# Another written-out order for the opening of a fused attention and SwiGLU kernel

## The chip, the cores and the metric

The kernel runs on one core of a Trainium2 chip. A core has a matrix engine (TensorE, PE in the profile; its weight loads are PEld), a vector engine (VectorE, DVE), a scalar engine (ScalarE, ACT), a general one (GpSimd, POOL) and a queue processor (SyncE, SP) that issues the transfers. Each engine takes its instructions in the order in which the program gives them and waits where one needs something that isn't there yet. Sixteen DMA engines move the data. The metric is the device time of one execution in microseconds, as the median of several runs.

## The reference

Windowed causal attention is followed by a gated feed-forward block, both in float32:

```python
batch, n_heads, seq, head_dim = (8, 8, 576, 64)
scores = scale * np.matmul(q, k.transpose(0, 1, 3, 2))
mask = (rel >= 0) & (rel < window)          # rel = query - key, window = 64
attn = exp(scores - max) / sum              # masked scores at -1e9
x = (attn @ v).transpose(0, 2, 1, 3).reshape(4608, 512)
g = x @ w_gate                              # 512 -> 1536
out = (g * sigmoid(g) * (x @ w_val)) @ w_out    # 1536 -> 512
```

q, k and v are 9.4 MB each, the three weight matrices 3.1 MB each.

## The kernel before

**Tiles.** The 4608 tokens are 36 groups of 128 (ORDER); four groups make a tile of 512 tokens, t = 0 to 8. A block n holds the q or k of groups 2n and 2n + 1; v is loaded by group. Weights come in slices s of 256 columns, wg and wv (gate and value) of 512 KB each; slice s serves the output blocks m = 2s and 2s + 1 of the hidden layer. All matrix work is in bf16, so every load is followed by a cast. Loads are named in short below: q3 is q of block 3, v4 is v of group 4, wg5 and wv5 are the gate and value slices 5, wo5 the output slice 5.

**The parts of a group.** `load` (L89), `load1` (L101) and `load_vg` (L110) issue loads of q, k and v; `cast_k` casts to bf16; `turn2` turns a block of q or k by 16 TensorE transposes (L170) and copies the result out of PSUM, `turn1` does it by DMA (L155). `scores` (L207) multiplies keys and queries; with masked=True it adds 16 matmuls that put a large negative number where the mask is off (L215), without it `weigh` has to multiply by a 0/1 mask on VectorE (L229) after the exponential on ScalarE (L227). `cast_v` makes three copies of a group's v: vo as it is, and ve shifted by half a group, which also serves the next group. `products` (L245) multiplies by v, `norm` divides by the row sums (L255, L256), `turn_x` transposes the result on TensorE (L269) and copies it into xT on ScalarE (L270); `turn_x1` does the same by DMA (L277).

**The feed-forward part.** `weights` (L284) and `weights_o` (L292) load slices, `cast_w` and `casts_o` cast them (L120 or L118, on the engine that is named). `step(t, m, c0, n)` computes hidden block m of tile t for n of its 512 tokens: four matmuls into g_ps, four into v_ps (L309), and tanh on ScalarE (L314). `finish()` takes the oldest open step and makes its hidden values on VectorE (L320, L321); only then are its two PSUM buffers free, and there are two of each. `project(t, s)` multiplies by w_out (L327) and stores 128 tokens. `warm(n)` issues n matmuls on zeros.

**What sets the order.** Nothing is planned at run time: the order of the calls is the order on each engine. The opening, some 250 calls written out one by one between `begin()` and the loop, brings in the weights, does the attention of the first groups and all of tiles 0 and 1 but the projection of tile 1. Behind it a loop over w works on tile t while it projects tile t - 1. All loads are issued by SP, so the order of the load calls is the order of the transfers. PSUM tiles of scores, products, transposes and projections rotate through four buffers (ps_a); staging has two buffers for each of q, k and v and six for weight slices.

Of the kernel before, what the change touches and what calls it, by code (L numbers as in the profile page):

```python
# [17 lines left out]
def kernel(  # L18
# [55 lines left out]
    dve, pool, act, sp = nc.vector, nc.gpsimd, nc.scalar, nc.sync  # L74
# [262 lines left out]
    def warm(n):  # L337
        w_ps = ps_f.tile([P, 512], FP32, name="w_ps", tag="g")
        for _ in range(n):
            nc.tensor.matmul(w_ps[:], wz[:, 0:P], wz[:])  # L340

    def begin():

        dve.memset(wz[:], 0.0)
        make_identity(nc, identb[:])
        dve.memset(masks[0][:], 1.0)
        dve.memset(minus[0][:], 0.0)
        pool.affine_select(
            out=masks[0][:], in_=masks[0][:], compare_op=ALU.is_ge, fill=0.0,
            base=64, pattern=[[0, 2], [1, 64]], channel_multiplier=-1,  # L350
        )
# [27 lines left out]
    begin()
    load(0, q, "q_f")  # L380
    load(0, k, "k_f")
    cast_k(0, "q_f", (act, dve))
    load(1, k, "k_f")
    load_vg(0)
    cast_k(0, "k_f", (act, pool))
    load_vg(1)
    warm(11)
    turn2(0, "q_f", (act, dve))
    warm(4)
    turn2(0, "k_f", (act, dve))  # L390
    cast_k(1, "k_f", (dve, act))
    warm(3)
    scores(1)
    load(1, q, "q_f")
    cast_v(0, (dve, pool, pool))
    scores(0, True)
    cast_k(1, "q_f", pool)
    load(2, k, "k_f")
    cast_v(1, (dve, None, None))
    weigh(1)  # L400
    load(2, q, "q_f")
    weigh(0)
    warm(6)
    products(0)
    load_vg(2)
    load_vg(3)
    weights(5, 0)
    load_vg(4)
    norm(0)
    keys_before(1)  # L410
    turn2(1, "k_f", (act, dve))
    warm(4)
    turn_x(0)
    turn2(1, "q_f", (act, dve))
    products(1)
    warm(1)
    scores(2, True)
    cast_k(2, "k_f", pool)
    norm(1)
    cast_k(2, "q_f", dve)  # L420
    weigh(2)
    warm(1)
    scores(3, True)
    weigh(3)
    weights(5, 1)
    load_vg(5)
    turn2(2, "q_f", act)
    load(3, k, "k_f")
    cast_v(2, (dve, pool, pool))
    keys_before(2)  # L430
    turn2(2, "k_f", dve)
    turn_x(1)
    warm(2)
    products(2)
    load(3, q, "q_f")
    norm(2)
    cast_v(3, (act, pool, pool))
    warm(1)
    scores(4, True)
    weights(0, 0)  # L440
    weigh(4)
    products(3)
    norm(3)
    cast_v(4, (act, pool, pool))
    warm(1)
    turn_x(2)
    warm(2)
    turn_x(3)
    weights(0, 1)
    scores(5, True)  # L450
    products(4)
    cast_w(5, 1, pool)
    cast_v(5, pool)
    weigh(5)
    cast_w(5, 0, dve)
    step(0, 10, 0, 256)
    norm(4)
    weights(4, 0)
    step(0, 10, 384, 128)
    turn_x(4)  # L460
    products(5)
    load_vg(6)
    finish()
    keys_before(3)
    cast_k(3, "k_f", (act, pool))
    weights(4, 1)
    norm(5)
    finish()
    step(0, 11)
    cast_k(3, "q_f", (dve, act))  # L470
    load_vg(7)
    turn_x(5)
    turn2(3, "k_f", (dve, act))
    turn2(3, "q_f", (act, dve))
    load(4, k, "k_f")
    cast_w(0, 0, pool)
    finish()
    step(1, 11, 0, 256)
    cast_w(0, 1, act)
    scores(6, True)  # L480
    load(4, q, "q_f")
    finish()
    load_vg(8)
    scores(7)
    step(0, 0)
    weigh(6)
    step(1, 0, 0, 256)
    cast_w(4, 0, pool)
    finish()
    finish()  # L490
    weigh(7)
    cast_w(4, 1, act)
    cast_v(6, pool)
    step(0, 1)
    cast_v(7, (act, pool, pool))
    products(6)
    step(0, 8)
    norm(6)
    cast_k(4, "k_f", (act, pool))
    products(7)  # L500
    turn_x(6)
    finish()
    norm(7)
    weights(3, 0)
    step(0, 9)
    cast_k(4, "q_f", (act, pool))
    cast_w(3, 0, pool)
    weights(1, 0)
    finish()
    weights(3, 1)  # L510
    weights(1, 1)
    keys_before(4)
    load_vg(9)
    finish()
    turn_x(7)
    cast_w(3, 1, pool)
    turn2(4, "k_f", (dve, act))
    turn2(4, "q_f", act)
    step(1, 8)
    finish()  # L520
    step(1, 1)
    weights(2, 0)
    load(5, q, "q_f")
    cast_w(1, 0, pool)
    finish()
    scores(8)
    cast_w(1, 1, pool)
    scores(9)
    weigh(8)
    weights_o(4)  # L530
    load(5, k, "k_f")
    step(1, 10)
    finish()
    cast_w(2, 0, pool)
# [12 lines left out]
    step(0, 7)
    cast_v(8, act)
    step(1, 3)
    finish()  # L550
    cast_k(5, "k_f", (act, pool))
    step(1, 9)
    cast_v(9, (dve, pool, pool))
    finish()
    cast_w(2, 1, pool)
    turn2(5, "q_f", act)
    step(0, 3)
    weights_o(2)
    load_vg(10)
    weights_o(0)  # L560
    finish()
    casts_o(1, pool)
    finish()
    step(0, 10, 256, 128)
    products(9)
    casts_o(4, pool)
    products(8)
    step(0, 4)
    norm(9)
    casts_o(5, pool)  # L570
    finish()
    finish()
    turn2(5, "k_f", act)
    cast_v(10, pool)
    load_vg(11)
    step(1, 2)
    norm(8)
    finish()
    weights_o(3)
    step(0, 5)  # L580
    load1(6, k, "k_f")
    casts_o(0, pool)
    load_vg(12)
    finish()
    scores(10)
    load(7, k, "k_f")
    scores(11)
    casts_o(2, pool)
    casts_o(3, dve)
    weigh(11)  # L590
    turn_x1(8)
    keys_before(6)
    weigh(10)
    cast_k(6, "k_f", pool)
    step(1, 7)
    step(1, 11, 256, 256)
    finish()
    turn_x(9)
    project(0, 3)
    cast_v(11, (pool, dve, act))  # L600
    load1(6, q, "q_f")
    turn1(6, "k_f")
    load1(7, q, "q_f")
    finish()
    cast_k(6, "q_f", (act, pool))
    turn1(6, "q_f")
# [114 lines left out]
```

The softmax here doesn't subtract the row's maximum and nothing guards it: scores larger than these inputs give would overflow.

## Time and profile before

| | |
|---|---|
| median of 4 runs | 339.31 us (338.38 to 339.42) |
| the profiled execution | 339.34 us, of which its span is 337.6 us |
| busy share of the span | PE 97%, PEld 48%, DVE 68%, ACT 45%, POOL 30% |
| SP's transfers | 56.51 MB on queue q1, 76.9% of 16 engines' span |
| TensorE clock | 0.999 of full |

The page divides the span into 40 slices with the busy share of each engine in tenths. The opening ends at 89 us, where the loop's first step starts; the loop fills the rest. "Idle before, releaser" says how long an engine waited ahead of an instruction and what let it go. The DMA share is the mean over 16 engines; where one engine is late and the others are done, it is small although a transfer is still running. A load's time to landing runs from the start of its issue on SP to the moment when whoever waits for it may go. Instructions themselves are fetched by DMA too, on queues of their own (q8, q14).

### The profile page before, as it was taken

How to read it: one execution, taken by the hardware profiler on the slowest of the kernel's cores; microseconds unless marked ns; L12 is line 12 of the kernel's file. 1: busy time of each engine (PE TensorE's matmuls, PEld its weight loads, DVE VectorE, ACT ScalarE, POOL GpSimd, SP SyncE). 2: the span in 40 equal slices, each digit the busy share in tenths (PEclk: the TensorE clock that was granted, in tenths of full speed). 3: DMA queues.
4: the chain of work that ended last, by engine and by line, in shares of the span. 5: the costliest groups of instructions: out<-in, count | busy, mean ns of one | idle time of the engine just before them, and what ended most of it. 6: DMA issues, size and time to landing. Idle time of an engine off the chain costs nothing.

```text
span 337.6 us, 7271 instructions
## 1 busy us (share of the span) xinstructions
PE 326.3 (97%) x2743; PEld 162.5 (48%) x2784; DVE 228.0 (68%) x486; ACT 150.9 (45%) x266; POOL 102.8 (30%) x150
## 2 busy tenths in 40 slices
PE   8887999999999999999999999999999999999996
PEld 3565554555444444444444444444444444444444
DVE  3786898896476767767676665866665866655520
ACT  3595866555534343434343434434343434233222
POOL 4354554842333333333333333223333110000000
PEclk9999999999999999999999999999999999999999
DMA  8999999969988989788989997999796520211014
GB/s 206 263 266 305 266 324 340 316 137 172 242 170 175 167 177 165 145 199 148 192 155 188 133 203 146 177 170 190 144 194 145 119 63 34 63 33 31 31 46 111
DMA packets 151155, 56.98 MB, mean 169 GB/s; under 512 B 125264, under 2 KB 145104, under 8 KB 151120
## 3 DMA queue, kind: packets, MB, share of 16 engines
q1 hardware_dynamic: 151120, 56.51, 76.9%
q8 instruction: 22, 0.36, 0.5%
q14 instruction: 13, 0.11, 0.1%
HBM read 37.75 MB, written 9.44 MB: 140 GB/s over the span
## 4 chain that ended last, share of the span: by engine, by line
PE 87%; DMA 8%; issue 1%; SPq 1%; POOL 1%; ACT 0%; DVE 0%; ACTq 0%; POOLq 0%
PE g_ps L309 27%; PE o_ps L327 27%; PE v_ps L309 27%; DMA v_f<-in_v_dram 4%; PE ao_ps L245 3%; DMA q_f<-in_q_dram 3%; PE s_ps L207 2%; SPq L89 1%; PE tp L170 1%; DMA kT<-k_fb 1%; DMA out_dram<-os__4939 1%; POOL ve L120 1%; PE xtp L269 0%; DVE sg L320 0%; ACT os__4939 L332 0%
## 5 line engine op out<-in xcount | busy, mean ns | idle before, releaser
L320 DVE SCALAR_TENSOR_TENSOR sg<-th,g_ps 128x512 f32<-128x512 f32 (+1 forms) x112 | 74.4, 664 | 56.8 <-ACT th L314 56.5
L309 PE MATMUL g_ps<-xT,wg 128*128 128x512 bf16 (+2 forms) x416 | 110.0, 372 | 2.0 <-DVE sg L320 0.3
L309 PE MATMUL v_ps<-xT,wv 128*128 128x512 bf16 (+2 forms) x445 | 110.9, 371 | 0.9 <-POOL wv L120 0.8
L314 ACT ACTIVATE th<-g_ps 128x512 f32<-128x512 f32 (+1 forms) x112 | 65.1, 584 | 77.5 <-PE g_ps L309 76.0
L327 PE MATMUL o_ps<-wo,hT 128*128 128x512 bf16 (+2 forms) x454 | 98.4, 368 | 0.2
L321 DVE TENSOR_TENSOR hT<-sg,v_ps 128x512 bf16<-128x512 f32 (+1 forms) x112 | 74.9, 669 | 12.4 <-PE v_ps L309 1.0
L309 PEld LDWEIGHTS <-wv 128*128 128x128 bf16 x448 | 43.4, 98 | 50.9 <-POOL wv L120 1.1
L327 PEld LDWEIGHTS <-hT 128*128 128x128 bf16 x456 | 43.6, 98 | 49.2
L309 PEld LDWEIGHTS <-wg 128*128 128x128 bf16 x448 | 40.9, 98 | 43.7 <-issue 0.3
L227 ACT ACTIVATE E<-s_ps 128x512 bf16<-128x512 f32 x72 | 38.8, 598 | 10.0 <-PE s_ps L207 8.6
L120 POOL CAST q_fb<-q_f 128x1024 bf16<-128x1024 f32 (+1 forms) x15 | 14.9, 991 | 70.0 <-DMA q_f<-in_q_dram 58.3
L120 POOL CAST k_fb<-k_f 128x1024 bf16<-128x1024 f32 (+1 forms) x17 | 15.9, 934 | 60.3 <-DMA k_f<-in_k_dram 55.7
L120 POOL CAST ve<-v_f 64x512 bf16<-64x512 f32 x49 | 30.7, 626 | 8.2 <-DMA v_f<-in_v_dram 5.4
L256 DVE TENSOR_TENSOR x_b<-ao_ps,r 128x256 bf16<-128x256 f32 x72 | 30.5, 424 | 2.5
L229 DVE TENSOR_TENSOR E<-E,mask 128x512 bf16<-128x512 bf16 x60 | 26.8, 478 | 7.9 <-ACT E L227 7.3
L120 POOL CAST vo<-v_f 128x512 bf16<-128x512 f32 x24 | 15.2, 633 | 6.2 <-DMA v_f<-in_v_dram 6.2
L245 PEld LDWEIGHTS <-E 128*64 128x64 bf16 x576 | 11.5, 110 | 8.3 <-issue 5.9
L255 DVE RECIPROCAL r<-ao_ps 128x4 f32<-128x4 f32 x72 | 12.5, 173 | 1.2 <-PE ao_ps L245 1.2
L207 PEld LDWEIGHTS <-kT 64*128 64x128 bf16 x512 | 9.9, 95 | 6.8 <-issue 3.4
L245 PE MATMUL ao_ps<-ve,E 128*64 128x65 bf16 x256 | 12.4, 196 | 0.4 <-POOL ve L120 0.2
L245 PE MATMUL ao_ps<-vo,E 128*64 128x65 bf16 x256 | 12.5, 196 | 0.0
L207 PE MATMUL s_ps<-qT,kT 64*128 64x64 bf16 x512 | 12.2, 191 | 0.3 <-ACT qT L118 0.3
(99 smaller groups left out, 149.0 us busy)
## 6 DMA issues: line engine op xcount, KB each, us to landing
v_f<-in_v_dram SPq DMA_DIRECT2D x32, 256.0 KB, 4.6
q_f<-in_q_dram SPq DMA_DIRECT2D x20, 256.0 KB, 4.4
k_f<-in_k_dram SPq DMA_DIRECT2D x18, 256.0 KB, 4.2
k_f<-in_k_dram SPq DMA_DIRECT2D x7, 512.0 KB, 6.9
q_f<-in_q_dram SPq DMA_DIRECT2D x6, 512.0 KB, 5.2
w_f<-in_moe_w_gate_dram SPq DMA_DIRECT2D x6, 512.0 KB, 7.5
w_f<-in_moe_w_val_dram SPq DMA_DIRECT2D x6, 512.0 KB, 7.6
wo_f<-in_moe_w_out_dram SPq DMA_DIRECT2D x6, 512.0 KB, 7.9
```

What stands on the lines that cost most here:

```text
L120: eng.tensor_copy(y, x)
L207: nc.tensor.matmul(ps[a][:, p, b], keys, qT[g // 2 % QR][y, p, o:o + 64], tile_position=(64 * a, 0), start=True, stop=not masked,)
L227: act.activation(e, x[:], AF.Exp, scale=0.125)
L229: dve.tensor_mul(e, e, mk[:].unsqueeze(1).to_broadcast([P, 4, 2, 64]))
L245: nc.tensor.matmul(o_ps[64 * b:64 * b + 64, i, :], Es[g % ER][:, y, b], z[:, y, :], tile_position=(0, 64 * b),)
L255: dve.reciprocal(r[:], o_ps[:, :, D])
L256: dve.tensor_mul(xb[g][:, 256 * h:256 * h + 256].rearrange("r (y d) -> r y d", y=4), o_ps[:, :, 0:D], r[:].unsqueeze(2).to_broadcast([P, 4 ...
L309: nc.tensor.matmul(ps[:, 0:n], w[:, c, P * m:P * m + P], xT[t][:, c, c0:c0 + n], start=(c == 0), stop=(c == 3),)
L314: act.activation(th[:, 0:n], g_ps[:, 0:n], AF.Tanh, scale=0.5)
L320: dve.scalar_tensor_tensor(sg[:, 0:n], th[:, 0:n], 1.0, g_ps[:, 0:n], ALU.add, ALU.mult)
L321: dve.tensor_mul(hT[t][:, m, c0:c0 + n], sg[:, 0:n], v_ps[:, 0:n])
L327: nc.tensor.matmul(o_ps[:, a:b], hT[t][:, c, P * s:P * s + P], wo[:, c, a:b], start=(c == 0), stop=(c == 11),)
```

## The change

The order of the opening is replaced. The functions, the loop, the tiles and all buffers stay as they were. In words:

- k of block 0 is loaded ahead of q; v of group 1 comes after q of block 1; v of group 2 ahead of q of block 2, which now comes ahead of k; later v6 and v7 stand each ahead of a weight slice; q4 ahead of k4; the last weight slices come in the order 2, 3, 1 (before: 3, 1, 2), the output weights and the loads of blocks 6 and 7 in another order too.
- Many casts and copies are put on other engines. Of the gate and value slices, wv0 and wv4 go from ScalarE to GpSimd and wg3 from GpSimd to ScalarE; the slices of the output weights are spread over ScalarE, VectorE and GpSimd.
- scores(1) and scores(7) get the mask, scores(6) loses it.
- Steps (1, 10) and (1, 1) are each done in two halves; several steps change places.
- Group 8 is turned by TensorE (`turn_x`) instead of by DMA (`turn_x1`).
- 34 warm matmuls instead of 36, in other places.

```diff
--- before.py
+++ after.py
@@ -377,253 +377,257 @@
         dve.memset(x[:, :, D:VW], 1.0)
 
 begin()
+load(0, k, "k_f")
+cast_k(0, "k_f", pool)
 load(0, q, "q_f")
-load(0, k, "k_f")
-cast_k(0, "q_f", (act, dve))
 load(1, k, "k_f")
+cast_k(0, "q_f", (dve, pool))
+warm(11)
+turn2(0, "k_f", (dve, act))
+warm(3)
+turn2(0, "q_f", (dve, act))
 load_vg(0)
-cast_k(0, "k_f", (act, pool))
+warm(3)
+scores(1, True)
+load(1, q, "q_f")
+scores(0, True)
+cast_k(1, "q_f", dve)
 load_vg(1)
-warm(11)
-turn2(0, "q_f", (act, dve))
+weigh(1)
+cast_k(1, "k_f", pool)
+cast_v(0, (act, pool, pool))
+weigh(0)
+warm(2)
+turn2(1, "k_f", (act, dve))
+load_vg(2)
+load(2, q, "q_f")
+cast_v(1, (dve, pool, pool))
 warm(4)
-turn2(0, "k_f", (act, dve))
-cast_k(1, "k_f", (dve, act))
-warm(3)
-scores(1)
-load(1, q, "q_f")
-cast_v(0, (dve, pool, pool))
-scores(0, True)
-cast_k(1, "q_f", pool)
+turn2(1, "q_f", (dve, act))
 load(2, k, "k_f")
-cast_v(1, (dve, None, None))
-weigh(1)
-load(2, q, "q_f")
-weigh(0)
-warm(6)
+load_vg(3)
 products(0)
-load_vg(2)
-load_vg(3)
+keys_before(1)
 weights(5, 0)
 load_vg(4)
+cast_v(2, (pool, act, act))
+warm(4)
+scores(2, True)
+weights(5, 1)
+weigh(2)
+load_vg(5)
+cast_k(2, "q_f", pool)
 norm(0)
-keys_before(1)
-turn2(1, "k_f", (act, dve))
-warm(4)
+load(3, k, "k_f")
+load(3, q, "q_f")
+products(1)
 turn_x(0)
-turn2(1, "q_f", (act, dve))
-products(1)
+weights(0, 0)
+norm(1)
+weights(0, 1)
+cast_k(2, "k_f", (dve, pool))
+cast_v(3, pool)
+warm(2)
+turn2(2, "q_f", act)
+keys_before(2)
+scores(3, True)
+load_vg(6)
 warm(1)
-scores(2, True)
-cast_k(2, "k_f", pool)
-norm(1)
-cast_k(2, "q_f", dve)
-weigh(2)
+products(2)
+weigh(3)
+norm(2)
 warm(1)
-scores(3, True)
-weigh(3)
-weights(5, 1)
-load_vg(5)
-turn2(2, "q_f", act)
-load(3, k, "k_f")
-cast_v(2, (dve, pool, pool))
-keys_before(2)
-turn2(2, "k_f", dve)
 turn_x(1)
-warm(2)
-products(2)
-load(3, q, "q_f")
-norm(2)
-cast_v(3, (act, pool, pool))
+turn2(2, "k_f", (act, dve))
+cast_w(5, 0, dve)
+weights(4, 0)
+turn_x(2)
+products(3)
 warm(1)
 scores(4, True)
-weights(0, 0)
+norm(3)
+cast_v(4, (pool, act, dve))
+cast_w(5, 1, pool)
+cast_v(5, pool)
+load_vg(7)
 weigh(4)
-products(3)
-norm(3)
-cast_v(4, (act, pool, pool))
-warm(1)
-turn_x(2)
 warm(2)
 turn_x(3)
-weights(0, 1)
 scores(5, True)
+weigh(5)
 products(4)
-cast_w(5, 1, pool)
-cast_v(5, pool)
-weigh(5)
-cast_w(5, 0, dve)
+keys_before(3)
 step(0, 10, 0, 256)
 norm(4)
-weights(4, 0)
+weights(4, 1)
 step(0, 10, 384, 128)
+finish()
 turn_x(4)
 products(5)
-load_vg(6)
-finish()
-keys_before(3)
-cast_k(3, "k_f", (act, pool))
-weights(4, 1)
+finish()
 norm(5)
-finish()
+cast_k(3, "k_f", pool)
 step(0, 11)
-cast_k(3, "q_f", (dve, act))
-load_vg(7)
+cast_k(3, "q_f", (act, dve))
+load(4, q, "q_f")
 turn_x(5)
-turn2(3, "k_f", (dve, act))
-turn2(3, "q_f", (act, dve))
+finish()
+turn2(3, "k_f", act)
+cast_w(0, 0, pool)
+turn2(3, "q_f", (dve, act))
+step(1, 10, 0, 256)
+step(1, 11, 0, 256)
+finish()
+scores(6)
+cast_w(0, 1, pool)
+finish()
+weigh(6)
+scores(7, True)
 load(4, k, "k_f")
-cast_w(0, 0, pool)
-finish()
-step(1, 11, 0, 256)
-cast_w(0, 1, act)
-scores(6, True)
-load(4, q, "q_f")
-finish()
+step(0, 1)
 load_vg(8)
-scores(7)
+step(1, 1, 0, 256)
+finish()
+finish()
+cast_w(4, 0, pool)
+weigh(7)
+weights(2, 1)
 step(0, 0)
-weigh(6)
+cast_v(6, (pool, act, act))
+keys_before(4)
+weights(3, 1)
 step(1, 0, 0, 256)
-cast_w(4, 0, pool)
-finish()
-finish()
-weigh(7)
-cast_w(4, 1, act)
-cast_v(6, pool)
-step(0, 1)
-cast_v(7, (act, pool, pool))
+cast_v(7, (pool, pool, act))
+cast_w(4, 1, pool)
+finish()
+cast_k(4, "q_f", act)
 products(6)
+products(7)
+norm(6)
+step(0, 9)
+finish()
+turn_x(6)
+norm(7)
+weights(2, 0)
 step(0, 8)
-norm(6)
-cast_k(4, "k_f", (act, pool))
-products(7)
-turn_x(6)
-finish()
-norm(7)
+cast_k(4, "k_f", pool)
+turn_x(7)
+cast_w(2, 1, pool)
+finish()
+turn2(4, "q_f", (dve, act))
+load_vg(9)
+cast_w(3, 1, pool)
 weights(3, 0)
-step(0, 9)
-cast_k(4, "q_f", (act, pool))
-cast_w(3, 0, pool)
+load(5, q, "q_f")
+cast_w(2, 0, pool)
+turn2(4, "k_f", act)
+cast_v(8, pool)
+step(1, 9)
 weights(1, 0)
 finish()
-weights(3, 1)
+finish()
+step(1, 8)
+step(1, 1, 256, 256)
+finish()
+scores(8)
 weights(1, 1)
-keys_before(4)
-load_vg(9)
-finish()
-turn_x(7)
-cast_w(3, 1, pool)
-turn2(4, "k_f", (dve, act))
-turn2(4, "q_f", act)
-step(1, 8)
-finish()
-step(1, 1)
-weights(2, 0)
-load(5, q, "q_f")
+scores(9)
+step(1, 11, 256, 256)
+finish()
 cast_w(1, 0, pool)
 finish()
-scores(8)
-cast_w(1, 1, pool)
-scores(9)
-weigh(8)
 weights_o(4)
 load(5, k, "k_f")
-step(1, 10)
-finish()
-cast_w(2, 0, pool)
+cast_w(1, 1, pool)
+weigh(9)
+step(1, 4)
+keys_before(5)
+weights_o(1)
+finish()
+cast_v(9, pool)
+cast_w(3, 0, act)
+step(0, 4)
+step(1, 5)
+finish()
+finish()
+cast_k(5, "q_f", (act, dve))
 step(0, 6)
-keys_before(5)
-weights(2, 1)
-finish()
-step(1, 6)
-finish()
+finish()
+load_vg(10)
 step(0, 2)
-weights_o(5)
-cast_k(5, "q_f", pool)
-finish()
-weights_o(1)
-weigh(9)
-step(0, 7)
-cast_v(8, act)
-step(1, 3)
-finish()
-cast_k(5, "k_f", (act, pool))
-step(1, 9)
-cast_v(9, (dve, pool, pool))
-finish()
-cast_w(2, 1, pool)
-turn2(5, "q_f", act)
+weights_o(3)
+finish()
+load_vg(11)
+weights_o(0)
+weigh(8)
 step(0, 3)
 weights_o(2)
-load_vg(10)
-weights_o(0)
-finish()
+finish()
+step(1, 2)
+cast_k(5, "k_f", pool)
+products(9)
+norm(9)
+finish()
+cast_v(10, (act, pool, pool))
+weights_o(5)
+load1(7, q, "q_f")
+load1(6, q, "q_f")
+casts_o(4, act)
 casts_o(1, pool)
-finish()
+products(8)
+step(0, 5)
+finish()
+norm(8)
+turn2(5, "k_f", act)
+turn2(5, "q_f", act)
+cast_v(11, pool)
+step(0, 7)
+finish()
+casts_o(3, pool)
+step(1, 3)
+scores(11)
+finish()
+scores(10)
+load1(6, k, "k_f")
+weigh(11)
+weigh(10)
+step(1, 10, 256, 256)
+load(7, k, "k_f")
+finish()
+turn_x(8)
+step(1, 7)
+products(11)
+casts_o(0, act)
+products(10)
+step(1, 6)
+load_vg(12)
+casts_o(5, dve)
+casts_o(2, pool)
+norm(11)
+project(0, 0)
+cast_k(6, "k_f", act)
+norm(10)
+finish()
+turn_x(9)
+keys_before(6)
+cast_k(6, "q_f", dve)
+turn1(6, "q_f")
+project(0, 1)
 step(0, 10, 256, 128)
-products(9)
-casts_o(4, pool)
-products(8)
-step(0, 4)
-norm(9)
-casts_o(5, pool)
-finish()
-finish()
-turn2(5, "k_f", act)
-cast_v(10, pool)
-load_vg(11)
-step(1, 2)
-norm(8)
-finish()
-weights_o(3)
-step(0, 5)
-load1(6, k, "k_f")
-casts_o(0, pool)
-load_vg(12)
-finish()
-scores(10)
-load(7, k, "k_f")
-scores(11)
-casts_o(2, pool)
-casts_o(3, dve)
-weigh(11)
-turn_x1(8)
-keys_before(6)
-weigh(10)
-cast_k(6, "k_f", pool)
-step(1, 7)
-step(1, 11, 256, 256)
-finish()
-turn_x(9)
-project(0, 3)
-cast_v(11, (pool, dve, act))
-load1(6, q, "q_f")
 turn1(6, "k_f")
-load1(7, q, "q_f")
-finish()
-cast_k(6, "q_f", (act, pool))
-turn1(6, "q_f")
-step(1, 5)
-products(11)
-norm(11)
-products(10)
-cast_k(7, "k_f", (dve, pool))
-step(1, 0, 256, 256)
-project(0, 0)
-norm(10)
-cast_v(12, (pool, act, act))
 turn_x(10)
 turn_x(11)
-finish()
-project(0, 1)
 load_vg(13)
+project(0, 3)
+load_vg(14)
+finish()
+cast_k(7, "k_f", dve)
+step(1, 0, 256, 256)
 finish()
 project(0, 2)
-load_vg(14)
+cast_v(12, (dve, pool, pool))
+turn2(7, "k_f", (dve, act))
 keys_before(7)
-step(1, 4)
-turn2(7, "k_f", act)
 load1(8, k, "k_f")
```

More of the change, by code (lines that the diff above doesn't have):

```diff
@@ L463 @@
     finish()
-    keys_before(3)
-    cast_k(3, "k_f", (act, pool))
-    weights(4, 1)
     norm(5)
-    finish()
-    step(0, 11)
-    cast_k(3, "q_f", (dve, act))
-    load_vg(7)
-    turn_x(5)
-    turn2(3, "k_f", (dve, act))
-    turn2(3, "q_f", (act, dve))
-    load(4, k, "k_f")
-    cast_w(0, 0, pool)
-    finish()
-    step(1, 11, 0, 256)
-    cast_w(0, 1, act)
-    scores(6, True)
-    load(4, q, "q_f")
-    finish()
-    load_vg(8)
-    scores(7)
-    step(0, 0)
-    weigh(6)
-    step(1, 0, 0, 256)
@@ L488 @@
-    cast_w(4, 0, pool)
+    cast_k(3, "k_f", pool)
+    step(0, 11)
+    cast_k(3, "q_f", (act, dve))
+    load(4, q, "q_f")
+    turn_x(5)
+    finish()
+    turn2(3, "k_f", act)
[9 more added lines that the diff above has]
+    scores(7, True)
+    load(4, k, "k_f")
+    step(0, 1)
+    load_vg(8)
+    step(1, 1, 0, 256)
     finish()
     finish()
+    cast_w(4, 0, pool)
@@ L491 @@
     weigh(7)
-    cast_w(4, 1, act)
-    cast_v(6, pool)
-    step(0, 1)
-    cast_v(7, (act, pool, pool))
-    products(6)
+    weights(2, 1)
+    step(0, 0)
+    cast_v(6, (pool, act, act))
+    keys_before(4)
+    weights(3, 1)
+    step(1, 0, 0, 256)
+    cast_v(7, (pool, pool, act))
+    cast_w(4, 1, pool)
+    finish()
+    cast_k(4, "q_f", act)
+    products(6)
+    products(7)
[5 more added lines that the diff above has]
+    weights(2, 0)
     step(0, 8)
-    norm(6)
@@ L533 @@
-    finish()
-    cast_w(2, 0, pool)
+    cast_w(1, 1, pool)
[3 more added lines that the diff above has]
+    weights_o(1)
+    finish()
+    cast_v(9, pool)
[5 more added lines that the diff above has]
+    cast_k(5, "q_f", (act, dve))
     step(0, 6)
-    keys_before(5)
-    weights(2, 1)
     finish()
-    step(1, 6)
+    load_vg(10)
+    step(0, 2)
+    weights_o(3)
     finish()
-    step(0, 2)
-    weights_o(5)
-    cast_k(5, "q_f", pool)
-    finish()
@@ L562 @@
+    weights_o(5)
+    load1(7, q, "q_f")
+    load1(6, q, "q_f")
+    casts_o(4, act)
     casts_o(1, pool)
+    products(8)
+    step(0, 5)
     finish()
-    step(0, 10, 256, 128)
-    products(9)
-    casts_o(4, pool)
-    products(8)
-    step(0, 4)
-    norm(9)
-    casts_o(5, pool)
-    finish()
-    finish()
-    turn2(5, "k_f", act)
-    cast_v(10, pool)
-    load_vg(11)
-    step(1, 2)
-    norm(8)
-    finish()
-    weights_o(3)
-    step(0, 5)
-    load1(6, k, "k_f")
-    casts_o(0, pool)
@@ L610 @@
-    products(10)
-    cast_k(7, "k_f", (dve, pool))
-    step(1, 0, 256, 256)
-    project(0, 0)
-    norm(10)
-    cast_v(12, (pool, act, act))
+    keys_before(6)
+    cast_k(6, "q_f", dve)
+    turn1(6, "q_f")
+    project(0, 1)
+    step(0, 10, 256, 128)
+    turn1(6, "k_f")
     turn_x(10)
     turn_x(11)
+    load_vg(13)
+    project(0, 3)
+    load_vg(14)
     finish()
-    project(0, 1)
-    load_vg(13)
+    cast_k(7, "k_f", dve)
+    step(1, 0, 256, 256)
     finish()
     project(0, 2)
-    load_vg(14)
+    cast_v(12, (dve, pool, pool))
```

## The prediction

> **What bounds the kernel now.** I read the busy table by stretches first, then the waits of TensorE, the chain that ended last, and SP's queue. The stretches of the opening (columns: stretch, length, busy of PE, PEld, DVE, ACT, POOL with counts, clock, DMA share, GB/s):
>
> ```profile
> 16.00:18.10 2.10, 1.72 (x65) 1.23 (x65) 1.30 (x5) 1.35 (x3) 1.04 (x1) 1.00 1.02 195
> 18.10:18.90 0.80, 0.36 (x7) 0.36 (x8) 0.44 (x2) 0.80 (x2) 0.00 (x0) 1.00 0.54 106
> 18.90:21.00 2.10, 2.01 (x35) 1.30 (x33) 2.10 (x4) 1.82 (x4) 1.94 (x3) 1.00 1.14 336
> 21.00:25.97 4.97, 3.86 (x111) 2.92 (x112) 4.51 (x14) 4.15 (x9) 2.96 (x5) 1.00 1.10 276
> 25.97:31.20 5.23, 4.18 (x51) 2.95 (x53) 3.05 (x11) 2.48 (x5) 2.45 (x4) 1.00 1.05 320
> 31.20:40.00 8.80, 8.55 (x110) 5.09 (x112) 7.43 (x17) 7.97 (x16) 5.16 (x7) 1.00 0.98 271
> 40.00:60.00 20.00, 19.84 (x152) 9.97 (x154) 18.36 (x34) 13.95 (x25) 9.83 (x11) 1.00 1.10 328
> 60.00:75.00 15.00, 14.89 (x151) 8.43 (x152) 13.65 (x29) 8.02 (x15) 9.91 (x11) 1.00 0.93 231
> ```
>
> From about 32 us TensorE is busy 99% of the time (19.84 of 20.00). Before that it isn't, and the DMA share is about 1 except in one hole: 0.54 at 18.1 to 18.9. So after 32 us the end is set by the amount of TensorE work left; before it, by when data lands. TensorE's last waits in the opening, by its timeline:
>
> ```profile
> 25.97 0.61 PE L309 MATMUL v_ps<-xT,wv 128*128 128x256 bf16 x4 [0.80 <-POOL wv L120]
> 31.20 0.46 PE L170 MATMUL tp<-identb,q_fb 128*128 128x128 bf16 x4 [0.84 <-DVE q_fb L120]
> 31.86 0.38 PE L170 MATMUL tp<-identb,q_fb 128*128 128x128 bf16 x4 [0.20 <-ACT xT L270]
> ```
>
> The last one is q of block 3 (q3): the chain that ended last goes through that very load, and from there through TensorE alone:
>
> ```profile
> 11.02 7.80 DMA v_f<-in_v_dram
> 21.70 8.92 DMA q_f<-in_q_dram
> 34.89 0.86 PE v_ps L309 x4
> ```
>
> **q3 lands at 30.6, and the whole rest follows it.** What the change can win is how much earlier TensorE starts on what comes after q3 (32.08 now); what it can lose is a new wait later.
>
> **The loads, in both orders.** Landings are issue start plus time to landing, or the start of the cast that waited. q0 5.2, k0 7.0, k1 8.9, v0 10.0, v1 11.2, q1 13.0, k2 15.9, q2 17.7, v2 18.8, wg5 21.4, v4 22.4, wv5 24.7, v5 25.9, k3 27.6, q3 30.6, wg0 32.0, wv0 33.5, wg4 35.1, v6 35.9, wv4 37.4, v7 38.5, k4 40.1, q4 42, v8 43. So a q or k costs 1.8, a v 1.1, a w 1.5. Three steps are longer: k2 2.9, wv5 2.3, q3 3.0. In front of each an instruction packet ran on queue q8 (starts at 12.5 to 13.0, 20.8 to 21.2, 26.0 to 26.5; 1.2, 1.2 and 1.9 us on one engine, from the queue's share of those stretches). [...]
>
> The new order has the same set of loads ahead of wv5 (13), of q3 (16) and of wv0 (18); only inside it v1 goes behind q1, v2 ahead of q2, and q2 ahead of k2. [...] If all engines are always fed, the same set ends at the same time: q3 at 30.6, gain nothing. But they are not always fed. SP's own queue:
>
> ```profile
> 11.02 4.85 SPq L110 DMA_DIRECT2D v_f<-in_v_dram  x2
> 15.91 1.60 SPq L284 DMA_DIRECT2D w_f<-in_moe_w_gate_dram  x1
> 17.69 0.38 SPq L110 DMA_DIRECT2D v_f<-in_v_dram  x1
> ```
>
> An unhindered issue takes 0.38; v2 and v3 took 4.85 together and wg5 1.60. SP is held until an older load has drained. In the hole I count by packet size 77 packets under 512 B from 18.0 to 18.9: one or two engines still finish v3, the others are idle, since wg5 (issued until 17.51) brings its first data only at 18.85, some 1.35 later. When wg5 was let in, only v2 and v3 were left, 2.2 us of work, less 1.2 of lag from the packet at 12.5: 1.0, under 1.35. In the new order k2 and v3 are left at that point: 2.9 - 1.2 = 1.7, above 1.35. **So the hole closes, worth 0.75.** Bounds: nothing (the late engine is the same for all three packets, so it never idled), 0.8 (the whole hole). I take 0.75, since the lead of the other engines at 18.9 was gone and so the later packets hit engines that had idled. q3 then lands at 29.85.
>
> **TensorE up to q3.** k0 first means that k0 is cast on POOL at 5.2 to 6.3 and q0 on DVE and POOL at 7.0 to 7.65; first scores at 8.95 (8.88 now). The mask of scores(1) adds 16 matmuls, in pairs at a pitch of 0.03, 0.24, and takes two DVE multiplies (0.76) away; both lie under waiting. v1 lands at 12.9 to 14.0 (11.2 now), and its DVE cast stands ahead of the copy of qT of block 1: qT is ready at 15.15 at the latest, scores(2) at 15.4 (16.04 now). q2's cast on POOL ends by 18.0, scores(3) at 18.5 (16.93 now: later, for it sits behind the transposes of q2). Then DVE: norm(2) to 21.1, kT half to 21.95, cast of wg5 (1.13) to 23.1, norm(3) (four operations, 1.05) to 24.15; TensorE: turn_x(3) 24.25, scores(5) 24.5, products(4) 25.15, step(0,10) g at 25.5, v at 25.95 (25.97 now). So the earlier wv5 brings nothing, this chain is then the bound, with no slack. On: 128 columns to 26.85, turn_x(4), products(5) to 27.45, step(0,11) (1.73) to 29.2, turn_x(5), turn2 of k3 to 29.85. q3 lands at 29.85, its cast on ACT takes 0.62: transposes at 30.5, done 30.95; xT of group 5 is copied right behind the cast, until 31.05. **TensorE starts the rest at 31.05 instead of 32.08: -1.03.**
>
> **What is left then** is the same list of work but for:
> - turn_x(8) on TensorE instead of the DMA transpose (L277, 1.53 of SP): four transposes, 0.23 by the others of this line (40.88 to 41.11). +0.23.
> - steps (1,10) and (1,1) in halves: a half takes 0.43 + 0.43 (32.08, 32.51), a whole 0.86 + 0.86. 0.00; one more th, sg and hT each, small and behind TensorE.
> - the mask moves from scores(6) to scores(7): 0. Two fewer warm matmuls (34 for 36): they fill waits, 0.
> - products(7) needs the upper v of group 7, cast on ACT with cast_v(6) behind th of step(0,0): ACT 39.1 to 40.3, TensorE there at 40.1. +0.25; bounds 0 and 1 (ACT's next two operations).
> - weight casts wv0 and wv4 go from ACT to POOL (1.05 and 1.04 each): POOL is free (5.16 busy of 8.80), wv0 is cast by 34.6 and needed at 35.5; wv4 lands behind v7 at 38.5 instead of 37.4, is cast by 39.95 after two casts of v7, and needed at 41.5. Cover 0.9 and 1.5. Then in the new order of slices wg2 lands at 47.8, needed 51.2; wg1 and wv1 by 56.1, needed 58.1. Without that cover each us is an us on the path. 0.
> - finish() in other places: g and v buffers (two each) come free 0.1 to 0.4 before they are asked for (step(0,0): sg at 37.0, asked at 37.05). 0.
> - block 6's k goes last to the DMA transpose, behind q's: on SP at 83 to 86 behind two output stores, landed by 88.5, needed at 91. 0.
>
> The sum is made against the profiled execution: 339.34, of which 337.6 is span and 1.74 lies around it; the runs' median is 339.31, so nothing is to be converted. 339.34 - 1.03 + 0.23 + 0.25 = 338.79, **338.8**.
>
> **Rivals.** A difference under 0.3% (1.0 us) can't be told from none here, the runs spread by 1.04.
> (1) The order moves nothing: the late engine is always the same and never idles, q3 stays at 30.6, TensorE starts the rest at 31.9 (the 0.20 for xT is gone). 339.34 - 0.2 + 0.23 + 0.25 = 339.6. For it: the three long steps add up to 3.1, nearly all that the packets took. Against: a packet at 35 to 36 lengthened no step.
> (2) Slower: a weight slice comes late. From 32 to 60 POOL carries nine slices, k4, v6 to v9 in program order, and what stands at its head holds all behind it. The place is step(0,1) or step(0,9); it decides once a cast ends more than 0.9 or 1.5 later than I have it. Slices at 2.3 or 3 us instead of 1.5, as with wv5, would do it: a wait of 1 to 2.5 on TensorE. 339.6 + 1.5 = 341.1. Against: DMA moves 271 to 328 GB/s there, and now no slice is late.
> (3) More gain: the hole closes and the packet at 26 finds an engine that is ahead, so q3 lands at 29.5; the chain through wg5's cast keeps up, and products(7) doesn't wait. The rest starts at 30.7: 339.34 - 1.4 + 0.23 = 338.2, and 337.9 where the lag of the packets falls on different engines. Against: the chain through wg5's cast has no slack.
>
> **How the numbers follow.** Forecast 0.34 (its own range 338.2 to 339.4), (1) 0.20, (2) 0.29, (3) 0.17. Faster than 338.3: most of (3) (0.14) and a third of the forecast (0.12), 0.26. Slower than 340.4: 0.27 of (2) and 0.03 of (1), 0.30. Within: 0.44. The range to leave out 2 in 10: 337.7 below (1 in 10, the whole gain and no new wait) to 341.1 above (half of (2) lies beyond).
>
> **What would show it.** Right: no stretch near 18 us with a DMA share of about 0.5; q_f of block 3 landed near 29.9; TensorE busy without a hole from about 31; turn_x(8) as four transposes. Wrong: q3 at 30.6 or later; a wait of TensorE on POOL wg or wv after 32; a hole of the DMA at another place ahead of q3; the first scores or step(0,10) over 1 us later than 8.95 and 25.5.

## The result and the profile after

The changed kernel takes 338.54 us (median of 42 runs, 337.88 to 340.27); the kernel before took 339.32 (median of 63, 338.23 to 341.82) beside it. The ratio is 0.9982 (95% interval 0.9975 to 0.9988), so about -0.6 us (-0.4 to -0.85); the plain medians differ by 0.78. The forecast was 338.8. The sum is near, but one of its steps isn't how it came about.

The profiled execution took 338.72, with a span of 337.0 (before: 339.34 and 337.6). Its opening by stretches (stretch, length, busy of PE, PEld, DVE, ACT and POOL, clock, DMA share, GB/s):

```profile
16.00:18.10 2.10, 0.74 (x5) 0.32 (x5) 0.44 (x2) 2.08 (x5) 0.90 (x2) 1.00 0.94 232
18.10:18.90 0.80, 0.41 (x6) 0.40 (x6) 0.00 (x0) 0.21 (x1) 0.35 (x1) 0.78 0.54 143
18.90:21.00 2.10, 2.10 (x41) 1.38 (x41) 0.99 (x2) 1.42 (x2) 1.71 (x3) 0.50 1.12 300
25.97:31.20 5.23, 5.18 (x86) 3.88 (x80) 4.89 (x15) 4.02 (x9) 3.43 (x5) 1.00 1.03 299
40.00:60.00 20.00, 19.84 (x158) 10.78 (x154) 17.60 (x36) 13.03 (x23) 10.63 (x14) 1.00 1.10 312
```

Three things are to be read here. The hole of the DMA at 18.1 to 18.9 is still there, at the same share, 0.54. From 26 on TensorE is full (5.18 of 5.23, where it was 4.18). And there is something new: TensorE did only 0.74 of work between 16 and 18.1, and then, by finer stretches, ran at half the clock (0.50) from about 18.5 to 22.

TensorE's timeline (start, length, operation, in brackets the idle time before it and what ended it) shows the cost of that and where it went:

```profile
17.30 0.38 PE L269 MATMUL xtp<-identb,x_b 128*128 128x128 bf16 x4 [1.77 <-ACT E L227]
...
18.50 1.02 PE L170 MATMUL tp<-identb,q_fb 128*128 128x128 bf16 x8 [0.39 <-POOL q_fb L120]
...
26.62 0.61 PE L309 MATMUL g_ps<-xT,wg 128*128 128x256 bf16 x4
27.07 0.60 PE L309 MATMUL v_ps<-xT,wv 128*128 128x256 bf16 x4
...
30.61 0.61 PE L170 MATMUL tp<-identb,k_fb 128*128 128x128 bf16 x8
31.05 0.61 PE L170 MATMUL tp<-identb,q_fb 128*128 128x128 bf16 x8
31.50 0.60 PE L309 MATMUL g_ps<-xT,wg 128*128 128x256 bf16 x4
```

step(0,10) starts at 26.62, where I had 25.5, and waits for nothing any more: wv5 had landed at 25.3. The transposes of q3 don't wait either: q3 had landed at 29.9, 1.15 before they start. The rest starts at 31.50 instead of 32.08. TensorE's waits in the first 95 us (tile and line, what ended them, sum, count, longest) hold no line for a weight slice, for q3 or for v of group 7. The waits on q_fb are all before 19 us, so they are of earlier blocks:

```profile
PE xtp L269 <- ACT E L227: 2.1, 2, 1.8
PE w_ps L340 <- DVE wz L344: 1.3, 1, 1.3
PE tp L170 <- POOL k_fb L120: 0.6, 1, 0.6
PE tp L170 <- POOL q_fb L120: 0.6, 2, 0.4
PE tp L170 <- DVE q_fb L120: 0.5, 1, 0.5
...
```

The chain that ended last no longer passes through the load of q3 but through that of q2, and from there through TensorE:

```profile
3.33 6.41 DMA v_f<-in_v_dram
9.73 7.52 DMA q_f<-in_q_dram
17.41 1.05 POOL q_fb L120
18.50 1.04 PE tp L170 x8
```

### The profile page after: what moved, and what is told of

Same layout as the page of the kernel before. It is cut to its first block, busy times and chain, and to the rows that moved or that the text cites. A ratio compares the mean times of both kernels' runs of the same rounds, so it can differ in the third digit from the quotient of the medians.

```text
span 337.0 us, 7337 instructions
## 1 busy us (share of the span) xinstructions
PE 326.2 (97%) x2776; PEld 164.9 (49%) x2818; DVE 224.6 (67%) x486; ACT 150.4 (45%) x265; POOL 103.8 (31%) x151
## 4 chain that ended last, share of the span: by engine, by line
PE 90%; DMA 5%; issue 1%; ACT 1%; SPq 1%; DVE 0%; POOL 0%; ACTq 0%; POOLq 0%; DVEq 0%
PE g_ps L309 28%; PE v_ps L309 27%; PE o_ps L327 27%; PE ao_ps L245 3%; PE s_ps L207 3%; DMA q_f<-in_q_dram 2%; DMA v_f<-in_v_dram 2%; PE tp L170 1%; PE xtp L269 1%; DMA kT<-k_fb 1%; SPq L89 1%; DMA out_dram<-os__4982 1%; POOL q_fb L120 0%; ACT qT L118 0%; PE w_ps L340 0%
## 5 line engine op out<-in xcount | busy, mean ns | idle before, releaser
L320 DVE SCALAR_TENSOR_TENSOR sg<-th,g_ps 128x512 f32<-128x512 f32 (+2 forms) x114 | 74.8, 656 | 54.8 <-ACT th L314 54.3
L314 ACT ACTIVATE th<-g_ps 128x512 f32<-128x512 f32 (+2 forms) x114 | 65.6, 576 | 78.6 <-PE g_ps L309 75.1
L321 DVE TENSOR_TENSOR hT<-sg,v_ps 128x512 bf16<-128x512 f32 (+2 forms) x114 | 75.2, 660 | 11.5
L309 PEld LDWEIGHTS <-wv 128*128 128x128 bf16 x456 | 44.3, 98 | 49.0
L309 PEld LDWEIGHTS <-wg 128*128 128x128 bf16 x456 | 41.6, 98 | 43.3
L120 POOL CAST k_fb<-k_f 128x1024 bf16<-128x1024 f32 (+1 forms) x16 | 17.0, 1061 | 55.7 <-DMA k_f<-in_k_dram 39.0
L256 DVE TENSOR_TENSOR x_b<-ao_ps,r 128x256 bf16<-128x256 f32 x72 | 30.5, 424 | 2.5
L120 POOL CAST q_fb<-q_f 128x1024 bf16<-128x1024 f32 (+1 forms) x13 | 13.4, 1029 | 59.7 <-DMA q_f<-in_q_dram 32.4
L229 DVE TENSOR_TENSOR E<-E,mask 128x512 bf16<-128x512 bf16 x58 | 22.7, 421 | 7.6 <-ACT E L227 7.0
L120 POOL CAST vo<-v_f 128x512 bf16<-128x512 f32 x28 | 17.4, 623 | 8.7 <-DMA v_f<-in_v_dram 8.5
```

What stands on the lines that cost most here:

```text
L120: eng.tensor_copy(y, x)
L229: dve.tensor_mul(e, e, mk[:].unsqueeze(1).to_broadcast([P, 4, 2, 64]))
L256: dve.tensor_mul(xb[g][:, 256 * h:256 * h + 256].rearrange("r (y d) -> r y d", y=4), o_ps[:, :, 0:D], r[:].unsqueeze(2).to_broadcast([P, 4 ...
L309: nc.tensor.matmul(ps[:, 0:n], w[:, c, P * m:P * m + P], xT[t][:, c, c0:c0 + n], start=(c == 0), stop=(c == 3),)
L314: act.activation(th[:, 0:n], g_ps[:, 0:n], AF.Tanh, scale=0.5)
L320: dve.scalar_tensor_tensor(sg[:, 0:n], th[:, 0:n], 1.0, g_ps[:, 0:n], ALU.add, ALU.mult)
```

## The experiments

Two explanations stood against each other: that the order of loads gives the gain by bringing q3 in earlier, and that the order only goes with the new division of work among the engines and moves no late landing. A third question was what the half clock costs. In what follows, times are medians, and ratios, with their 95% intervals, are to the kernel before on the same chip. What is read from a trace is read from one execution.

**The order of loads alone** (v1, q1, k2, q2 and v2), in the kernel before:

```diff
     cast_k(0, "k_f", (act, pool))
+    load(1, q, "q_f")
     load_vg(1)
...
     scores(1)
-    load(1, q, "q_f")
...
-    load(2, k, "k_f")
+    load_vg(2)
...
     load(2, q, "q_f")
+    load(2, k, "k_f")
...
     products(0)
-    load_vg(2)
     load_vg(3)
```

> The kernel before with one part of the change alone: q1 ahead of v1, v2 ahead of q2, q2 ahead of k2; all else, k0 and q0 too, as before. Theory A (the order of the loads is what brings q3 earlier): q3 lands near 29.9 instead of 30.6, TensorE turns it by 30.6 to 31.0, and the time falls by 0.4 to 0.8 to 338.5 to 338.9. Theory B (where an instruction packet falls decides when q3 lands, the order of the loads doesn't): q3 lands at 30.6 within 0.3 and the time is 339.3 within 0.3, or above that where v1 and k2, which now land later, hold up VectorE.

Measured: 339.99, ratio 1.0014 (1.0001 to 1.0027): no gain, rather a loss. q3 landed at 30.4. The old code wants v1 early, since norm(0) stands behind its cast on VectorE; v1 now landed at 13.0, and TensorE waited for it. Its timeline:

```profile
15.59 0.29 PE L269 MATMUL xtp<-identb,x_b 128*128 128x128 bf16 x2 [2.13 <-DVE x_b L256]
```

After that wait the clock was 0.50 from 16 to 19.4. So the order of loads isn't the source of the gain by itself; in the old division of work it makes a new wait, and q3 landed no earlier for it than in other traces.

**The old order of loads**, in the changed kernel:

```diff
     scores(1, True)
+    load_vg(1)
     load(1, q, "q_f")
...
-    load_vg(1)
     weigh(1)
...
-    load_vg(2)
+    load(2, k, "k_f")
     load(2, q, "q_f")
...
-    load(2, k, "k_f")
+    load_vg(2)
     load_vg(3)
```

> The changed kernel with the old order of v1, q1, k2, q2, v2, v3, everything else changed. Theory A: q3 lands at 30.6 again, TensorE waits for it and starts the rest at 32.0, 0.5 later than the changed kernel: 339.0 to 339.2. Theory B: q3 lands at 29.9 as in the changed kernel, and the time is 338.5 within 0.3, less if q2's later landing doesn't matter, more by up to 0.6 if the chain through q2 (now 0.5 later) sets the time.

Measured: 342.5, ratio 1.0087 (1.0062 to 1.0112). The order matters very much to the changed kernel, but not by q3, which landed at 29.8 here, as early as in the new order. It matters since ScalarE casts v2 ahead of the exponentials of group 2, and v2 lands at 18.8 in the old order. ScalarE's timeline, and TensorE's behind it:

```profile
18.81 1.26 ACT L118 CAST ve<-v_f 64x512 bf16<-64x512 f32 x2 [3.94 <-DMA v_f<-in_v_dram]
19.98 1.07 ACT L227 ACTIVATE E<-s_ps 128x512 bf16<-128x512 f32 x2
```

```profile
20.61 0.59 PE L269 MATMUL xtp<-identb,x_b 128*128 128x128 bf16 x4 [3.90 <-ACT E L227]
```

This is also the shape of the 1.77 in the changed kernel: the same cast waits 1.80 for v2 there.

**TensorE kept busy in that wait**: seven more filler matmuls in the changed kernel.

```diff
     products(1)
+    warm(7)
     turn_x(0)
```

> The changed kernel with seven more warm matmuls (1.5 us) in the wait of 1.77 us ahead of turn_x(0). Theory C (the matrix clock falls to 0.50 from 18.1 to 21 because TensorE idles there, and that lengthens the chain from q2 to step(0,10)): the clock stays at 1.00, the transposes of q2 take 0.62 instead of 1.02, step(0,10) begins 0.4 to 0.6 before 26.6, the time falls by 0.2 to 0.5 to 338.0 to 338.3. Rival D (the chain is set by landings and casts, the slow stretch lies under waiting): step(0,10) begins at 26.6 within 0.2, the time is 338.5 within 0.2.

Measured: 338.30, ratio 0.9964 (0.9953 to 0.9976). The clock stayed at 1.00, the transposes of q2 took 0.62 instead of 1.02, and step(0,10) started at 25.30 instead of 26.62. But then TensorE waits for wv5, and shortly for q3, and the rest starts at 31.43, hardly earlier. Its timeline:

```profile
26.51 0.61 PE L309 MATMUL v_ps<-xT,wv 128*128 128x256 bf16 x4 [0.60 <-POOL wv L120]
30.95 0.62 PE L170 MATMUL tp<-identb,q_fb 128*128 128x128 bf16 x8 [0.17 <-ACT q_fb L118]
```

So the half clock costs the chain 1.3, nearly all of which lies under the landings.

**A shorter chain without the filler**: q2 is cast by VectorE and GpSimd together, and its transposes come right behind that, ahead of the cast of k2.

```diff
-    cast_k(2, "q_f", pool)
     norm(0)
...
     weights(0, 1)
+    cast_k(2, "q_f", (dve, pool))
+    warm(2)
+    turn2(2, "q_f", (dve, act))
     cast_k(2, "k_f", (dve, pool))
     cast_v(3, pool)
-    warm(2)
-    turn2(2, "q_f", act)
     keys_before(2)
```

> The changed kernel with the cast of q2 in two halves on VectorE and GpSimd instead of whole on GpSimd (0.61 for 1.04) and the copy of its transposes in two halves on VectorE and ScalarE instead of whole on ScalarE (0.69 for 1.01). If the chain from q2's landing to step(0,10) is what sets the changed kernel's time: step(0,10) begins 0.6 to 0.8 before 26.6, TensorE reaches q3's transposes at 30.4 and waits there for its cast (30.8 at best), the time falls by 0.2 to 0.3 to 338.2 to 338.3. If q3's landing sets it: step(0,10) earlier, the start of q3's transposes unmoved at 31.05, the time 338.5 within 0.2.

Measured: 338.75, ratio 0.9976 (0.9962 to 0.9991), as the change itself. In its trace the half clock remained, so that step(0,10) started at 26.28, only 0.34 earlier; wv5 landed at 26.0, and the rest started at 31.62.

**Both kernels a second time**, one execution each, to see how much of the traces belongs to the single execution:

> The kernel before, unchanged, for a second trace. If the landing of q3 and TensorE's wait for it belong to the kernel: q3 lands at 30.6 within 0.2, TensorE waits 0.7 to 1.1 for it, starts the rest at 32.0 to 32.2 and the loop at 88.9 to 89.1. If they differ from execution to execution: q3 anywhere from 29.8 to 30.6, and the 0.6 between the two traces is in part chance.

> The changed kernel, unchanged, for a second trace. If its gain belongs to the kernel: TensorE reaches q3's transposes at 30.9 to 31.2 without waiting for q3, starts the rest at 31.4 to 31.6, the clock is 0.50 in 18.9 to 21 again, q3 lands at 29.9 within 0.2. If it is chance: a wait for q3, or a start of the rest off by more than 0.3.

Before: 338.61, span 336.9. Its hole was deeper (share 0.38), wv5 landed at 25.7 instead of 24.7, and q3 early enough that nothing waited for it. Its timeline:

```profile
26.83 0.61 PE L309 MATMUL v_ps<-xT,wv 128*128 128x256 bf16 x4 [1.62 <-POOL wv L120]
...
30.43 0.61 PE L170 MATMUL tp<-identb,k_fb 128*128 128x128 bf16 x8
30.88 0.81 PE L170 MATMUL tp<-identb,q_fb 128*128 128x128 bf16 x8
31.53 0.60 PE L309 MATMUL g_ps<-xT,wg 128*128 128x256 bf16 x4
```

After: 338.23, span 336.5. Here the clock didn't fall, though TensorE was as idle (0.81 of 2.10), and no hole showed (share 0.97). Its timeline:

```profile
25.33 0.61 PE L309 MATMUL g_ps<-xT,wg 128*128 128x256 bf16 x4
25.78 0.60 PE L309 MATMUL v_ps<-xT,wv 128*128 128x256 bf16 x4
...
29.32 0.61 PE L170 MATMUL tp<-identb,k_fb 128*128 128x128 bf16 x8
30.61 0.62 PE L170 MATMUL tp<-identb,q_fb 128*128 128x128 bf16 x8 [0.68 <-ACT q_fb L118]
31.09 0.60 PE L309 MATMUL g_ps<-xT,wg 128*128 128x256 bf16 x4
```

That is the predicted walk (25.5, 25.95, 30.5, 31.05) within 0.2. But with a share of 0.97 q3 landed at 29.9, as it did with 0.54: so in these two executions the hole didn't set q3's landing.

**Group 8 turned by the DMA again**, in the changed kernel:

```diff
-    turn_x(8)
+    turn_x1(8)
```

> The changed kernel with group 8 turned by DMA as before. If the four transposes on TensorE cost what the sum gave them: 0.23 less, 338.3. If the DMA's issue (1.5 on SP between the loads of block 7 and v12) pushes something back that is waited for: 338.5 or more.

Measured: 339.61, ratio 0.9998 (0.9982 to 1.0014), where the changed kernel has 0.9982 and, in a second timing, 0.9975: no gain, and probably a loss. The trace shows a new wait. One tile fewer is taken from the ring of four PSUM tiles, so every later user gets another of them, and project(0,1) waits for one that norm is still reading. The timeline of TensorE:

```profile
78.92 2.76 PE L327 MATMUL o_ps<-wo,hT 128*128 128x512 bf16 x12 [0.55 <-DVE x_b L256]
```

From the start of the rest to the loop's first step it took 57.51, against 57.01 in the changed kernel; no other wait of TensorE is new, so the DMA's issue on SP held up nothing that TensorE waited for there.

**Filler and DMA transpose together** (the last two edits on the changed kernel at once):

> Both: seven more warm matmuls ahead of turn_x(0), and group 8 turned by DMA. If the two gains add: 0.24 and 0.23 below the changed kernel, 338.0 to 338.1. If not: 338.3.

Measured: 339.31, ratio 1.0006 (0.9983 to 1.0028), against 0.9964 (0.9953 to 0.9976) with the filler alone. Here the intervals are apart, so turning group 8 by DMA does lose. Its trace has the same wait of project(0,1), now 0.83. The step that I had costed at +0.23 is worth keeping.

**The new turn of block 3 alone**, in the kernel before:

```diff
-    turn2(3, "k_f", (dve, act))
-    turn2(3, "q_f", (act, dve))
+    turn2(3, "k_f", act)
+    turn2(3, "q_f", (dve, act))
```

> The kernel before with one part of the change alone, at q3: the transposes of k3 go into one PSUM tile that ScalarE copies, those of q3 are copied by VectorE and ScalarE in this order. In the kernel before the second half of q3's transposes waits 0.20 for a PSUM tile that ScalarE still reads; with one tile fewer that wait can't be. If the way from q3's landing to the rest (1.46 and 1.5 in the two traces of before, 1.2 in the changed kernel where it waits for q3) is part of the gain: the rest starts 1.2 to 1.3 behind q3's landing and the time falls by 0.2 to 0.3 to 339.0 to 339.1. If not: 339.3 within 0.15.

Measured: 339.38, ratio 0.9997 (0.9982 to 1.0013), so -0.1, give or take 0.5. The trace is of an execution that isn't typical: 342.95, 3.6 above the median. In it the clock was 0.50 from 27.59 to 31.00, and the rest starts at 33.37, 1.29 later than in the first trace of before. Behind the slow stretch, at full clock, q3's transposes take 0.45 (32.92 to 33.37) without the wait of 0.20 for xT: the saving is there, and too small for the times to show.

**Half of q3's load**, in the kernel before: four of the eight heads are loaded and cast twice, so this kernel leaves out half of that load.

```diff
+        a = 4 if (n, nm) == (3, "q_f") else H
         sp.dma_start(
-            x_f[:].rearrange("r h c d -> r h (c d)"),
-            src[b, :, s:s + 256, :].rearrange("h (r c) d -> r h (c d)", c=2),
+            x_f[:, 0:a].rearrange("r h c d -> r h (c d)"),
+            src[b, 0:a, s:s + 256, :].rearrange("h (r c) d -> r h (c d)", c=2),
         )
```

> The kernel before, but q3 is loaded for four of its eight heads only (the other four are left out; the cast takes the first four twice), so that q3 and all loads behind it land 0.9 earlier. If the landing of q3 sets the time of the kernel before: TensorE's wait of 0.84 goes, the rest starts 0.7 to 0.9 earlier, the time falls by 0.6 to 0.9 to 338.4 to 338.7. If the chain of the attention or the landing of wv5 is as near (as in its second trace): the fall is 0.2 to 0.5, to 338.8 to 339.1.

Measured: 338.79, ratio 0.9986 (0.9969 to 1.0002), so -0.5, give or take 0.55: a fall isn't certain. In the trace q3 isn't waited for any more, but wv5 (landed at 25.5) is, and the rest starts at 31.43. Its timeline (the lines of this kernel are shifted by nine):

```profile
26.63 0.61 PE L318 MATMUL v_ps<-xT,wv 128*128 128x256 bf16 x4 [1.36 <-POOL wv L121]
```

So in the kernel before, q3 is one of two binding loads: with it out of the way wv5 binds.

**The changed kernel and the filler once more**, on one chip:

> The changed kernel again, beside the next one on the same chip: 0.7 to 0.9 below the kernel before.

> The changed kernel with seven more warm matmuls again. If the fall of the matrix clock, which came in one of the two traces of the changed kernel and not in the other, costs time in part of its executions: 0.2 to 0.4 below the changed kernel in the median, and a smaller spread. If q3's landing is next in any case: 0.1 or less.

Measured: 338.52, ratio 0.9975 (0.9963 to 0.9987), and 338.33, ratio 0.9963 (0.9951 to 0.9976). The filler's lead by the medians was 0.24 the first time and is 0.19 now (0.6 and 0.4 by the ratios); the intervals overlap. The mean clock of each timed execution says how often it fell. In the changed kernel it is 0.990 to 0.995 in 29 of 43 executions (median 338.66) and 0.999 or 1.000 in the other 14 (338.40); the second time 0.994 or 0.995 in 12 of 22 (338.80), full in 10 (338.48). With the filler it is 0.998 or more in all 29. So a fall goes with some 0.3 us, on few executions, and the filler takes away about what it costs.

In the filler's trace q3 landed at 31.1, later than in any other. TensorE's waits:

```profile
PE tp L170 <- ACT q_fb L118: 1.6, 1, 1.6
PE xtp L269 <- ACT E L227: 0.2, 1, 0.2
```

The wait at 17 is down to 0.2, and the landing takes the gain back in this execution. The trace of the changed kernel (q3 at 29.2) shows the half clock again and the rest at 31.44.

## Why the prediction was near, and where it was wrong

**Step "the hole closes, worth 0.75, q3 then lands at 29.85": this one failed.** q3 landed at 29.9 in the profiled execution, but not for that reason. Over the traces where its landing can be read, it is, in the old order of loads, 30.6, about 30.0, 29.8 and 30.4 (mean 30.2); in the new one, 29.9, 29.9, 29.2, 30.4, 30.1, 30.3, 29.8, 30.1 and 31.1 (mean 30.1). wv5: 24.7, 25.7, 24.1, 26.2 and 25.5 (25.2) against 25.3, 24.3, 24.8, 26.0, 25.4, 26.0, 25.4, 25.7 and 24.6 (25.3). The means differ by 0.1, while landings within one order spread by up to 2. From so few traces, of kernels that differ in more than the order, a shift of half a microsecond can't be excluded; the 0.75 that I had claimed isn't seen. The first trace's 30.6 was one draw from that spread (the last section shows what was late in it), and I priced the change as if it were fixed. The hole is smaller on average in the new order (0.54 to 0.97, against 0.38 to 0.73), but q3 lands at 29.9 with a share of 0.54 and of 0.97. What I had set down for engines that are always fed, and set aside, fits better: the same set of loads ends at about the same time (q3 at 30.2 and 30.1, wv5 at 25.2 and 25.3 in the mean), gain nothing. Rival (1) was right in that; its reason, a late engine that never idles, wasn't tested, and its 339.6 is too high.

The trace of before doesn't bear out the sum behind the 0.75 either. Of its packets from 18.0 to 18.9, 68 are of 1024 B and so wg5's, the first at 18.21: the data comes 0.7 behind the end of its issue, not 1.35. That is less than the 1.0 of work that I had left for the other loads, so by my own sum there should have been no hole. And that SP is held until an older load has drained fits the two issues of that sum (v3's ended at 15.87, k2 landed at 15.9; wg5's at 17.51, q2 at 17.7), but k1's issue took 1.53, to 3.46, and ended before any load had landed (q0 at 5.2).

**The term -1.03 for the start of the rest** measured -0.58 and -0.44 between like traces; the means are 31.80 (two traces of before) and 31.34 (three of after), -0.46. One part has a mechanism: from q3's landing to the rest took 1.48 in the first trace of before and 1.19 in the second of the changed kernel, where q3 binds as well, -0.29; elsewhere q3's turn takes 0.45 instead of 0.65, -0.2. More traces bear this out. Where q3 isn't waited for and the clock holds, the way from v of step(0,10) to the rest took 4.62 to 4.80 in the code of before (three traces: its second, and those with the new loads and with half of q3) and 4.43 to 4.50 in the changed code (five: two of the changed kernel, the shorter chain, group 8 by DMA, filler and DMA together). My sum held this part too (30.6 to 32.08, 29.85 to 31.05). What is left of the -0.46, some 0.2, may be where the landings happened to fall in these executions.

**The walk along TensorE** held where the clock held (the second trace of the changed kernel). It left out the clock: I counted TensorE's waiting near 17 us as nothing, and two fewer filler matmuls as 0. In two of three traces of the changed kernel the half clock put step(0,10) at 26.62 and 26.50, over 1 us later, which I had named as a sign of being wrong. It cost little, some 0.3 in the timed executions where it fell, since the wait for wv5 (0.80 in the first trace of before) would have been there instead.

**+0.23 for turn_x(8) and +0.25 for products(7)**, together 0.48: from the start of the rest to the loop's first step both traces of before took 56.91, those of the changed kernel 57.01, 57.00 and 57.00, so +0.10. products(7) waited for nothing, and the DMA experiment shows that turning group 8 on TensorE avoids a wait rather than only costing 0.23.

**The steps at 0** (halved steps, masks, weight casts on GpSimd, finishes, block 6) held: no wait on a weight slice after 32 us, so rival (2) didn't come. Rival (3) neither: the chain was later than I had it.

**The sum again, by what was measured**: -0.46 + 0.10 = -0.36 by the traces, and the mean spans agree: 337.25 before (two), 336.90 after (three), -0.35. The timed ratio is worth -0.6 (-0.4 to -0.85), the second timing -0.85 (-0.45 to -1.25). So a quarter to a half of a microsecond isn't assigned to any step, and with so few traces against landings that spread by 2, it can't be. Two errors of about half a microsecond with opposite signs made the forecast look better than its reasoning: that its number came out so near was luck.

## What to carry to other kernels

An order of loads and the order of work on each engine are one plan: the order alone cost about 0.5 us (0.0 to 0.9), and the changed kernel with the old order was about 3 slower than the kernel before, so judge them together. A single trace gives one draw of when a queued load lands (q3 at 29.2 to 31.1 in the new order); before pricing a gain on a landing, look at a second execution, and ask which load binds next. A ring of buffers is shared state: taking one use out of it moves all later ones, and can make a wait further on (0.55 at 78.92, where turn_x(8) had stood at 71.29). Seven filler matmuls in a wait of 1.8 us kept the clock at full in all 29 executions: such a wait is worth filling where the clock would fall behind it (0.24 and 0.19 by the medians here, with intervals that overlap).

## What was not expected of the hardware

**The clock falls after a thin stretch, in some executions, and the traces show in which.** With TensorE busy for 0.74 of 2.10 us (one wait of 1.77), the granted clock was then 0.50 from 18.55 to 21.96, which is 3.41 us. In the traces of the changed opening without the filler it fell at 18.4 to 19.0 in four of five; the fifth, as thin, kept 1.00. With the filler it kept 1.00 in all three. In every trace the clock changes only at multiples of 3.41 us from its first record (that record is at 4.89 in the profiled execution, so 18.55 is four steps on; at 4.39 in the second trace of the changed kernel). The busy time of TensorE by windows on this grid, first in the profiled execution, then in that second trace:

```profile
15.13:18.55 3.42, 1.21 (x22) 0.67 (x16) 1.15 (x5) 2.79 (x5) 1.65 (x2) 1.00 0.90 231
18.55:21.96 3.41, 3.08 (x58) 2.35 (x60) 1.47 (x4) 2.10 (x3) 2.46 (x4) 0.50 1.01 250
...
14.63:18.04 3.41, 1.92 (x54) 1.27 (x54) 1.82 (x7) 2.73 (x5) 1.54 (x3) 1.00 1.16 256
18.04:21.46 3.42, 3.04 (x70) 2.31 (x71) 2.11 (x6) 2.55 (x6) 2.21 (x5) 1.00 1.11 280
```

So the same thin stretch lies in one window in the first, and has the busy time ahead of it in its window in the second. In the 13 traces that have a record of the clock, each window in which TensorE was busy for 1.67 us or less (seven in the openings, five at the kernel's end) was followed by a clock of 0.50, and none with 1.74 or more was. So in these traces the limit lies between 1.67 and 1.74 of 3.41 us, near half of the window.

**One order of loads lands 2 us apart** from one execution to the next (q3 from 29.2 to 31.1). Instruction packets on their own queue (q8) took 0.9 to 2.2 us each, and where they start moved too: over the 14 traces the first of them started at 11.8 to 14.1, the next at 20.5 to 25.9, the third at 25.8 to 31.9. The three longest go with late landings: 2.2 us at 26.5 with q3 at 31.1; 2.1 us at 21.6 (the trace with the new turn of block 3) with wv5 at 26.2, the latest of all; 1.9 us at 26.2 (the first trace of before) with q3 at 30.6, the latest of the old order.

What makes q3 late can be counted in the traces' records of single DMA packets. q3 moves in 1024 packets of 512 B, the weight slices behind it in packets of 1024 B. In the first trace of before up to 156 of the 512 B packets end in 0.25 us (up to 165 in the first of the changed kernel). There each of the last six quarters of a microsecond before q3 is complete has only 9 to 12 of them, about the share of one engine in sixteen, while the others are at the next slices already. Four fifths of q3 had moved by 27.6 there, no later than elsewhere (27.2 to 28.6 in 13 traces), but the last packet ended 2.5 us behind that; in the trace with q3 at 31.1 it was 2.6 us, in the other eleven 1.2 to 2.1. So in those two executions one late engine set the landing, whatever the order of the loads. That an instruction packet made it late fits the lengths but is argued: the records don't name the engine, and no run removed a packet.
